# Gated activations of 27 chunks transposed by DMA instead of by TensorE

## The chip, the cores and the metric

The kernel runs on one core of a Trainium2 chip. The metric is the device time of one execution in microseconds (us), lower is better. Three executions of the kernel before took 380.42, 380.49 and 380.88 us, median 380.49.

## The reference

Attention with spatially reduced keys, and behind it a mixture of eight low-rank adapters. Cut to what matters:

```python
B, C, H, W = 4, 128, 384, 32             # q: (B, 12288, 128), kv: (B, 384, 32, 128)
kv_pool = kv.reshape(B, H//4, 4, W//4, 4, C).mean(axis=(2, 4))
k = v = kv_pool.reshape(B, -1, C) @ w_sr                       # 768 keys a batch
a = softmax(q @ k.T / sqrt(C))
x = (a @ v).reshape(-1, C)                                     # 49152 tokens
logits = x @ w_gate                                            # 8 experts
# the two best experts of a token get softmax weights w; for each of them:
x += w * ((x @ A[e]) @ B[e])                                   # rank 16
```

## The kernel before, in words

**Tiles.** The 49152 tokens are worked on in 96 chunks of 512 (24 a batch). A chunk's scores are three units, each two matmuls of 128x512 into a tile `sg` and one exponential on ScalarE into `em` (L294). The attention product is 24 matmuls into `acc`; the routing logits come out of the same matmuls as extra columns of the values. VectorE normalizes into `xn` (reciprocal L315, product L320) and finds the best two logits (L340); GpSimd forms the gates `gw` (L352 to L368) with a tanh on ScalarE (L365).

**The adapters of one chunk.** All eight experts' low-rank matrices are taken together as one 128x128 matrix. A chunk's `xn` is transposed on TensorE into `tt_ps` and copied by VectorE to `tts` (L389, function `transposes`); `down` multiplies it into `h_ps`; `gate` multiplies by the gates on VectorE into `hg` (L420); `hg` is transposed in turn, in the other half of the same `tt_ps`, in the next slot; `up` multiplies it into `d_ps`; `finish` adds `xn` on VectorE into `osb` (L433) and issues the output's DMA on the SP queue (L434). Four matmuls each for a transpose, `down` and `up`. `tt_ps`, `h_ps`, `d_ps` and the tiles of the key preparation share two PSUM buffers (`mtile`).

**Slots.** After an opening written out by hand, one loop runs over slots k = 8 to 95. Slot k does the three score units of chunk k, attends chunk k-1, normalizes the chunk attended before, and, for the one chunk x that *enters* (`enter[k]`, x = k-4 in the slots concerned), the transposes of `xn` and the down-projection. `kh` holds the chunk whose gated activations are transposed in this slot (it entered a slot ago), `ku` the one that gets its up-projection (it entered two slots ago). The order in a slot is that of the code, kept on every engine's queue.

**What `begin(k)` issues.** On the SP queue the transposing load of 2048 queries, `load_qT` (L90), in the slots of `loads` (10, 14, 18, ... 62, then 61 and 63 to 67 for the last batch's groups); on GpSimd's queue the cast of a group of queries to bf16 in DRAM, `cast_q` (L80, tile `qbf`), in the slots of `casts` (8, 12, 15, 16, 19, 20, 23, 24, 28, ...); and on SP the loads of the next batch's keys, `load_kv` (L102), in slots 3 to 14 of the first batch and 0 to 11 of the second and third.

**The late chunks.** Chunks 68 to 89 already have both transposes done by DMA: GpSimd narrows `xn` to bf16 (L403), the gate writes beside it, and one DMA transpose on SP (`turn_dma`, L407, tile `turn`) turns both.

The times at which slots 14 to 18 start their score units in the trace are some 3.6 to 4.1 us apart; the name "slot 18" below is that of k = 18 (normalization at 86.22 us).

Of the kernel before, what the change touches and what calls it, by code (L numbers as in the profile page):

```python
# [11 lines left out]
BF16 = mybir.dt.bfloat16  # L12
# [8 lines left out]
def kernel(  # L21
# [10 lines left out]
    nc = tc.nc  # L32
    P = 128
# [6 lines left out]
    S = T // P  # L40
# [5 lines left out]
    NB = N // T  # L46
# [11 lines left out]
    gpool = ctx.enter_context(tc.tile_pool(name="gpool", bufs=6))  # L58
    run = ctx.enter_context(tc.tile_pool(name="run", bufs=3))
    opool = ctx.enter_context(tc.tile_pool(name="opool", bufs=8))  # L60
    qdram = ctx.enter_context(tc.tile_pool(name="qdram", bufs=1, space=bass.MemoryType.DRAM))
    ps_s = ctx.enter_context(tc.tile_pool(name="ps_s", bufs=2, space=bass.MemoryType.PSUM))
    ps_a = ctx.enter_context(tc.tile_pool(name="ps_a", bufs=1, space=bass.MemoryType.PSUM))
# [2 lines left out]
    keep = tc.keep_in_program_order  # L66

    def mm(*a, **k):
        return keep(nc.tensor.matmul(*a, **k))  # L69

    def mtile(shape, dtype=FP32, name="mb"):
        return ps_m.tile(shape, dtype, tag="mb", name=name)
# [10 lines left out]
    def load_qT(g):  # L83
        if g < B * NG - GC:
            t = qpool.tile([P, GT], BF16, tag="qT", name="qT")
        else:
            if "q" not in spare:
                spare["q"] = kvpool.tile([P, 4, 2, 4 * C], FP32, tag="kvr", name="qTs")
            t = spare["q"][:, g % GC].rearrange("p x c -> p (x c)").bitcast(BF16)
        keep(nc.sync.dma_start(t.rearrange("c (j p) -> c j p", p=P),  # L90
                               q_bf[g].rearrange("(p j) c -> p (j c)", p=P), transpose=True))
        qT[g] = t
# [190 lines left out]
    tts, xT, hgT, hp, hg, dp = {}, {}, {}, {}, {}, {}  # L283
    R = J // 2

    def scores(k, r):
        b = k // NB
        if k not in em:
            em[k] = ppool.tile([P, J, T], FP16, tag="em", name="em")
        rhs = qT[k // GC][:, (k % GC) * T:(k % GC + 1) * T]  # L290
        ps = ps_s.tile([P, 2, T], FP32, tag="sg", name="sg")
        for i in range(2):
            mm(ps[:, i], kfT[b][:, 2 * r + i], rhs, start=True, stop=True)
        keep(nc.scalar.activation(em[k][:, 2 * r:2 * r + 2], ps, AF.Exp, bias=0.0, scale=scale))  # L294
# [31 lines left out]
    SOLO, TURN = NCHUNK - 6, NCHUNK - 28  # L326
    sizes = [1, 1] + [2] * (TURN // 2 - 1) + [1] * (NCHUNK - TURN)
    by_dma = range(TURN, SOLO)
# [66 lines left out]
    def strip(t, i):  # L395
        if "t" not in spare:
            t_ = kvpool.tile([P, 4, 2, 4 * C], FP32, tag="kvr", name="turn")
            spare["t"] = t_.rearrange("p r x c -> p (r x c)").bitcast(BF16).rearrange(
                "p (n t h s c) -> p n t h s c", n=4, t=2, h=2, s=S)
        return spare["t"][:, t % 4, i]  # L400

    def narrow(k, t):
        keep(nc.gpsimd.tensor_copy(strip(t, 0)[:, 0], xn[k][:, :, 0:C]))  # L403

    def turn_dma(t, *what):
# [3 lines left out]
        for i, (d, k) in enumerate(what):  # L409
            d[k] = strip(t, 1)[:, lo + i]  # L410

    def down(k):
        hp[k] = mtile([P, S, P], name="h_ps")
        for s in range(S):
            mm(hp[k][:, s], xT[k][:, s], a_bf, start=(s == 0), stop=(s == S - 1))

    def gate(k, into=None):
        k0, m = first[k], k - first[k]
        hg[k] = run.tile([P, S, P], BF16, tag="hg", name="hg") if into is None else into
        keep(nc.vector.tensor_tensor(  # L420
            hg[k].rearrange("p s (e r) -> p (s e) r", e=E),
            hp[k].rearrange("p s (e r) -> p (s e) r", e=E),
            gw[k0][:, m * S:(m + 1) * S].rearrange("p s e -> p (s e)")
            .unsqueeze(2).broadcast_to([P, S * E, RK]), op=ALU.mult))
# [33 lines left out]
    def unit(k=None, r=None):  # L458
        k, r = units.pop(0 if k is None else units.index((k, r)))
        scores(k, r)  # L460
# [3 lines left out]
    loads = {4 * g - 6: g for g in range(4, 18)}  # L464
    loads.update({61: 20, 63: 21, 64: 18, 65: 22, 66: 19, 67: 23})
    assert len(casts) == B * NG - 4

    def begin(k):
        nonlocal sums, rest
        b, i = divmod(k, NB)  # L470
        g = k // GC
        if k in loads:
            load_qT(loads[k])
        if k in casts:
            cast_q(4 + casts.index(k))
        if b + 1 < B:
            lo = 3 if b == 0 else 0
            if i == lo:
                sums, rest = prepare(b + 1, nc.gpsimd)
                sums = sum(sums, [])  # L480
            if lo <= i < 12 + lo:
                load_kv(b + 1, (i - lo) // 4, (i - lo) % 4, None)
        if k == 7:
            for _ in range(2):
                sums.pop(0)()
# [11 lines left out]
    enter, t, left = {}, 1, list(range(NCHUNK - 3))  # L497
    while left:
        can = [k for k in left if ready[k] <= t]
        enter[t] = can[:2] if t == SOLO + 2 else can[:1]  # L500
        left = [k for k in left if k not in enter[t]]
        t += 1

    kh, ku, kd, kdone = [], [], [], []
    engines = {"DVE": nc.vector, "ACT": nc.scalar, "POOL": nc.gpsimd}
# [40 lines left out]
    kh, ku = enter[k1 - 1], enter[k1 - 2]  # L546
    for k in range(k1, NCHUNK):
        b, i = divmod(k, NB)
        ka = att.get(k, [])
        kx = enter.get(k, [])  # L550
        begin(k)

        def after_norm(kn):
            top(kn)
            if kn == first[kn] + size[kn] - 1:
                route(first[kn])

        kn = [n for n in att.get(k - 1, []) if normed[n] == k]
        unit()
        if kx and not kd and all(x_ in by_dma for x_ in kx):  # L560
            down(kx[0])
            todo = []
            for n in kn:
                normalize(n)
                if n in by_dma:
                    narrow(n, k)
                    todo = [(xT, n)]
            tanhs()
            for h_ in kh:
                if h_ not in by_dma:  # L570
                    transposes(None, h_, nc.vector)
            unit()
            gate(kx[0], strip(k, 0)[:, 1])
            todo.append((hgT, kx[0]))
            if len(kx) == 1:
                turn_dma(k, *todo)
            for u_ in ku:
                up(u_)
                finish(u_)
            attend(ka[0], 0)  # L580
            attend(ka[0], 1)
            unit()
            for n in kn:
                after_norm(n)
            attend(ka[0], 2)
            for x_ in kx[1:]:
                down(x_)
                gate(x_, strip(k, 0)[:, 0])
                turn_dma(k, (hgT, x_), *todo)
            attend(ka[0], 3)  # L590
            kh, ku = kx, kh
            continue
        tanhs()
        for x_ in kd:
            down(x_)
        for n in kn:
            normalize(n)
            if n in by_dma:
                narrow(n, k)
                turn_dma(k, (xT, n))  # L600
        px, ph = ([c for c in ks if c not in by_dma] for ks in (kx, kh))
        pairs = [(px[j] if j < len(px) else None, ph[j] if j < len(ph) else None)
                 for j in range(max(len(px), len(ph)))]
        for x_, h_ in pairs[:1]:
            transposes(x_, h_, nc.vector)
        for x_ in kd:
            gate(x_)
        unit()
        for u_ in ku:
            up(u_)  # L610
            finish(u_)
        for a_ in ka[:-1]:
            for s in range(S):
                attend(a_, s)
            normalize(a_)
            after_norm(a_)
        if ka and len(ka) == 1:
            attend(ka[0], 0)
        for n in kn:
            after_norm(n)  # L620
        if k >= 13:
            unit()
            n0 = 1
        else:
            attend(ka[0], 1)
            n0 = 2
        for x_ in kx[:1]:
            down(x_)
            gate(x_)
        kd = []  # L630
        if rest and i in ((14, 15, 16, 18, 19, 20, 21, 22, 23) if b == 0 else (11, 12, 13, 17, 18, 19, 21, 22, 23)):
            rest.pop(0)()
        for a_ in ka[-1:]:
            for s in range(n0 if len(ka) == 1 else 0, S):
                if s == S - 1:
                    for x_, h_ in pairs[1:]:
                        transposes(x_, h_, nc.scalar)
                        kd = [x_] if x_ is not None else []
                attend(a_, s)
        ku = kh  # L640
        kh = kx[:1] + kdone
        kdone = kd
        if b + 1 < B and i % 2 == 0 and (8 if b == 0 else 6) <= i <= 20:
            for _ in range(4 if (b, i) == (0, 18) else 3):
                sums.pop(0)()
# [185 lines left out]
```

## Time and profile before

| what | value |
|---|---|
| runs, median (lowest to highest) | 380.49 us (380.42 to 380.88) |
| profiled execution, span from the first to the last instruction | 379.1 us |
| median less that span | 1.4 us |
| ScalarE, GpSimd busy | 293.3 us (77%), 217.8 us (57%) |
| DMA moved | 82.22 MB, mean 217 GB/s |
| DMA queue of SP (q1), share of 16 engines | 69.8% |
| DMA queue of GpSimd's casts (q0) | 17.0% |

The profile is of one execution, and its times are counted from the first instruction; for that execution no device time apart from its span is listed, so the runs' median stands beside it. Each engine runs its own instructions in order. "L69" is a helper's line through which every matmul goes, so TensorE's rows are told apart by their tiles. SP only issues DMAs; its rows give how long an issue held it, and "to landing" is the time from the start of the issue until all data has arrived.

### The profile page before, as it was taken

To read this page: it belongs to the slowest core of one execution; us is meant where nothing else is said; L and a number is where in the kernel's file an instruction comes from. 1 tells how busy PE (TensorE), PEld (TensorE's weight loads), DVE (VectorE), ACT (ScalarE), POOL (GpSimd) and SP (SyncE) were. 2 spreads that over 40 slices of the span, in tenths; PEclk is the share of its full clock that TensorE was granted. 3 is DMA by queue.
4 is the path that set the end of the run, shared out by engine and by line. 5 is a ranking of instruction groups with operands and counts; after the bars stand their busy time and mean duration, and the time that the engine had idled before them with its cause. 6 is when DMAs were issued, how large, how long until landed. Compare 5 with 4: busy or idle time off the path is not lost.

```text
span 379.1 us, 11473 instructions
## 1 busy us (share of the span) xinstructions
PE 368.8 (97%) x4448; PEld 292.5 (77%) x4448; DVE 307.6 (81%) x925; ACT 293.3 (77%) x368; POOL 217.8 (57%) x493
## 2 busy tenths in 40 slices
PE   8899999999999999999999999999999999999993
PEld 5577788788788887878788887878787777777782
DVE  1447799998989889898989888898988777777785
ACT  1448986776878788787878787777778999999873
POOL 0120468878732387777833267777675666666442
PEclk9999999999999999999999999999999999999998
DMA  7988979999999998997898998989955867777623
GB/s 247 388 291 151 279 184 266 340 224 241 152 213 228 299 278 268 255 235 165 171 201 226 288 239 245 306 233 198 217 137 140 169 163 153 150 205 168 141 86 140
DMA packets 93863, 82.22 MB, mean 217 GB/s; under 512 B 73104, under 2 KB 73872, under 8 KB 93456
## 3 DMA queue, kind: packets, MB, share of 16 engines
q1 hardware_dynamic: 92672, 69.75, 69.8%
q0 software_dynamic: 704, 11.54, 17.0%
q8 instruction: 35, 0.57, 0.6%
q10 hardware_dynamic: 432, 0.20, 0.2%
q14 instruction: 20, 0.16, 0.2%
HBM read 50.53 MB, written 36.70 MB: 230 GB/s over the span
## 4 chain that ended last, share of the span: by engine, by line
PE 91%; DMA 4%; DVE 2%; issue 1%; ACT 1%; SPq 0%; POOL 0%; ACTq 0%; DVEq 0%; POOLq 0%
PE acc L69 35%; PE sg L69 32%; PE tt_ps L69 8%; PE d_ps L69 5%; PE h_ps L69 5%; DMA kvr<-in_kv_dram 4%; PE kpT_ps L69 2%; PE v_ps L69 1%; DVE kvr L135 1%; DVE xn L320 1%; PE kfT_ps L69 1%; DMA out_dram<-osb 1%; PE qT_ps L69 0%; SPq L102 0%; PE tail_ps L69 0%
## 5 line engine op out<-in xcount | busy, mean ns | idle before, releaser
L294 ACT ACTIVATE em<-sg 128x1024 f16<-128x1024 f32 x288 | 282.4, 1022 | 66.8 <-PE sg L69 64.1
L69 PE MATMUL acc<-vx,em 128*128 128x136 f16 x2280 | 166.5, 223 | 0.0
L69 PEld LDWEIGHTS <-em 128*128 128x128 f16 x2304 | 145.2, 98 | 7.7 <-DVE xn L320 0.4
L69 PE MATMUL sg<-qT,kfT 128*128 128x512 bf16 x480 | 142.1, 379 | 0.8 <-ACT em L294 0.7
L320 DVE TENSOR_TENSOR xn<-acc,rinv 128x540 f32<-128x540 f32 x95 | 68.4, 720 | 3.3
L69 PEld LDWEIGHTS <-tts 128*128 128x128 bf16 x564 | 43.0, 98 | 31.6 <-issue 0.4
L223 POOL TENSOR_TENSOR kvr<-kvr 128x512 f32<-128x512 f32 x54 | 67.3, 1270 | 0.1
L352 POOL TENSOR_TENSOR over<-xn,srt 128x64 f32<-128x64 f32 (+1 forms) x120 | 30.9, 278 | 55.4 <-DVE srt L340 55.3
L433 DVE TENSOR_TENSOR osb<-d_ps,xn 128x512 f32<-128x512 f32 x91 | 62.5, 688 | 0.0
L420 DVE TENSOR_TENSOR hg<-h_ps,gw 128x512 bf16<-128x512 f32 x71 | 49.0, 691 | 6.3 <-POOL gw L368 1.2
L389 DVE COPY tts<-tt_ps 128x1024 bf16<-128x1024 bf16 (+1 forms) x73 | 49.0, 672 | 0.0
L69 PEld LDWEIGHTS <-kfT 128*128 128x128 bf16 x576 | 45.3, 98 | 2.7 <-issue 1.0
L315 DVE RECIPROCAL rinv<-acc 128x4 f32<-128x4 f32 x95 | 17.3, 182 | 36.9 <-PE acc L69 35.9
L367 POOL TENSOR_TENSOR gw<-th,over 128x64 f32<-128x64 f32 (+1 forms) x60 | 17.3, 288 | 49.6 <-ACT th L365 47.4
L69 PEld LDWEIGHTS <-xn 128*128 128x128 bf16 x296 | 22.5, 98 | 16.7 <-DVE xn L320 0.4
L340 DVE MAX8 srt<-xn 128x8 f32<-128x8 f32 x380 | 34.4, 152 | 0.1
L69 PE MATMUL sg<-qTs,kfT 128*128 128x512 bf16 x96 | 28.6, 379 | 0.0
L69 PE MATMUL tt_ps<-id_bf,xn 128*128 128x128 bf16 x284 | 27.4, 219 | 0.0
L69 PE MATMUL h_ps<-a_bf,tts 128*128 128x128 bf16 x284 | 27.4, 219 | 0.0
L69 PE MATMUL tt_ps<-id_bf,hg 128*128 128x128 bf16 x280 | 27.1, 219 | 0.0
L69 PE MATMUL d_ps<-b_bf,tts 128*128 128x128 bf16 x276 | 26.7, 219 | 0.1
L358 POOL TENSOR_SCALAR over<-over 128x64 f32<-128x64 f32 (+1 forms) x60 | 19.8, 330 | 5.4
(93 smaller groups left out, 280.7 us busy)
## 6 DMA issues: line engine op xcount, KB each, us to landing
out_dram<-osb SPq DMA_DIRECT2D x94, 256.0 KB, 4.3
kvr<-in_kv_dram SPq DMA_DIRECT2D x45, 512.0 KB, 7.8
qbf<-in_q_dram POOLq DMA_DIRECT2D x22, 512.0 KB, 7.7
qf<-in_q_dram SPq DMA_DIRECT2D x8, 256.0 KB, 7.4
kvr<-in_kv_dram SPq DMA_DIRECT2D x6, 256.0 KB, 7.8
out_dram<-osb SPq DMA_DIRECT2D x3, 128.0 KB, 2.3
turn<-turn SPq DMA_TRANSPOSE x23, 3.1
qT<-qbf SPq DMA_TRANSPOSE x18, 7.4
```

What stands on the lines that cost most here:

```text
L69: return keep(nc.tensor.matmul(*a, **k))
L223: keep(adder.tensor_tensor(u[:, lo:hi], u[:, lo:hi], v[:, lo:hi], op=ALU.add))
L294: keep(nc.scalar.activation(em[k][:, 2 * r:2 * r + 2], ps, AF.Exp, bias=0.0, scale=scale))
L315: keep(nc.vector.reciprocal(ri, acc[k][:, :, VC]))
L320: keep(nc.vector.tensor_tensor(x[:, :, 0:VC], acc[k][:, :, 0:VC], ri.unsqueeze(2).broadcast_to([P, S, VC]), op=ALU.mult))
L340: keep(nc.vector.max(srt[k0][:, m, s], xn[k][:, s, C:C + E]))
L352: keep(eng.tensor_tensor(d, lg, so[:, :, i].unsqueeze(2).broadcast_to([P, n, 8]), op=ALU.subtract))
L358: keep(eng.tensor_scalar(mask, mask, 0.0, None, op0=ALU.is_ge))
L367: keep(eng.tensor_tensor(w[:, 0:n], th, mask, op=ALU.mult))
L389: keep(nc.vector.tensor_copy(sb[:, lo:hi], ps[:, lo:hi]))
L420: keep(nc.vector.tensor_tensor(hg[k].rearrange("p s (e r) -> p (s e) r", e=E), hp[k].rearrange("p s (e r) -> p (s e) r", e=E), gw[k0][:, m ...
L433: keep(nc.vector.tensor_tensor(osb, dp[k], xn[k][:, :, 0:C], op=ALU.add))
```

## The change

In 27 slots (13 to 23 of the first batch, 37 to 47 of the second, 61 to 65 of the third) the chunk that enters gets its gated activations turned by a DMA of its own, `turn_h_dma`, issued on SP right behind the gate, from a tile `hs` into a tile `ht` (a pool of four each). TensorE's transposes of `hg` and their half of VectorE's copy fall away for them. Their up-projection moves from the slot k+2 to k+3 (`late_up`), with the addition and the output behind it. A query load of such a slot is issued behind this transpose, at the end of the slot; in the other slots it goes from ahead of to behind the key load and the first score unit.

```diff
+    hpool = ctx.enter_context(tc.tile_pool(name="hpool", bufs=4))
...
+    def turn_h_dma(k):
+        hgT[k] = hpool.tile([P, S, P], BF16, tag="ht", name="ht")
+        keep(nc.sync.dma_start(hgT[k].rearrange("c s p -> c s p"),
+                               hg[k].rearrange("p s c -> p (s c)"), transpose=True))
...
-    def begin(k):
+    def begin(k, queries=True):
...
-        if k in loads:
+        if k in loads and queries:
             load_qT(loads[k])
...
+    by_queue = [k for t in range(8, TURN - 2) if t % NB >= 13 for k in enter[t]]
+    late_up = {}
...
-        begin(k)
+        begin(k, False)
...
         unit()
+        if k in loads and not any(x_ in by_queue for x_ in kx):
+            load_qT(loads[k])
+        ku = ku + late_up.pop(k, [])
...
-        px, ph = ([c for c in ks if c not in by_dma] for ks in (kx, kh))
+        px = [c for c in kx if c not in by_dma]
+        ph = [c for c in kh if c not in by_dma and c not in by_queue]
...
             down(x_)
-            gate(x_)
+            if x_ in by_queue:
+                gate(x_, hpool.tile([P, S, P], BF16, tag="hs", name="hs"))
+                turn_h_dma(x_)
+                late_up[k + 3] = [x_]
+                if k in loads:
+                    load_qT(loads[k])
+            else:
+                gate(x_)
...
-        ku = kh
+        ku = [c for c in kh if c not in by_queue]
```

More of the change, by code (lines that the diff above doesn't have):

```diff
@@ L590 @@
             attend(ka[0], 3)
-            kh, ku = kx, kh
+            kh, ku = kx, [c for c in kh if c not in by_queue]
             continue
```

## The prediction

> **What bounds the kernel now.** I read the page first, then the timeline of one slot on TensorE and VectorE, then the DMA answers. The page's own rows for the engines and for the transposes that the change takes away:
>
> ```profile
> span 379.1 us, 11473 instructions
> PE 368.8 (97%) x4448; PEld 292.5 (77%) x4448; DVE 307.6 (81%) x925; ACT 293.3 (77%) x368; POOL 217.8 (57%) x493
> L69 PE MATMUL tt_ps<-id_bf,hg 128*128 128x128 bf16 x280 | 27.1, 219 | 0.0
> ```
>
> TensorE is busy for 97% of the span, but a matmul's duration (219 ns) is its way through the array and overlaps its neighbours, so the price of an edit is read from starts. One slot on TensorE (slot 18, start us, then duration):
>
> ```profile
> 85.80 0.59 PE L69 MATMUL sg<-qT,kfT 128*128 128x512 bf16 x2
> 86.24 0.39 PE L69 MATMUL tt_ps<-id_bf,xn 128*128 128x128 bf16 x4
> 86.46 0.39 PE L69 MATMUL tt_ps<-id_bf,hg 128*128 128x128 bf16 x4
> 86.68 0.59 PE L69 MATMUL sg<-qT,kfT 128*128 128x512 bf16 x2
> 87.11 0.39 PE L69 MATMUL d_ps<-b_bf,tts 128*128 128x128 bf16 x4
> ...
> 89.64 0.59 PE L69 MATMUL sg<-qT,kfT 128*128 128x512 bf16 x2
> ```
>
> Each group starts when the one before has been fed; no gap stands between them. The four transposes of gated activations run from 86.46 to 86.68: 0.22 us, not the 0.39 of their row. The slot lasts 89.64 - 85.80 = 3.84 us. In the late slots, where both kinds of transposes already go by DMA, the same slot start recurs after 3.16 us, and ScalarE's three exponentials fill about that much:
>
> ```profile
> 297.87 0.59 PE L69 MATMUL sg<-qT,kfT 128*128 128x512 bf16 x2
> 301.03 0.59 PE L69 MATMUL sg<-qT,kfT 128*128 128x512 bf16 x2
> 299.54 3.15 ACT L294 ACTIVATE em<-sg 128x1024 f16<-128x1024 f32 x3
> ```
>
> So ScalarE would limit a slot at about 3.16. The plain slot at the start of the second batch lasts 3.61 (120.58 less 116.97, quoted further down). One transpose group less makes 3.39: still TensorE's, and 0.22 is really won per slot. VectorE's copy in slot 18 of the transposes (first row) shrinks by the half that went away, so VectorE, 81% busy, does not become the bound:
>
> ```profile
> 86.88 0.69 DVE L389 COPY tts<-tt_ps 128x1024 bf16<-128x1024 bf16 x1
> 87.54 0.69 DVE L433 TENSOR_TENSOR osb<-d_ps,xn 128x512 f32<-128x512 f32 x1
> ```
>
> **The change part by part.** The chunks that enter in slots 13-23, 37-47 and 61-65 are 11 + 11 + 5 = 27.
>
> Removed: 27 groups of transposes by 0.22 = 5.9 us, all on the path, in slots 14-24, 38-48 and 62-66.
>
> Added on TensorE: nothing, but the up-projection comes three slots after the chunk's down-projection instead of two. So slots 15, 39 and 63 have none and slots 26, 50 and 68 have two. The second one there needs the PSUM buffer that the transposes used, which is free when VectorE has copied them. In slot 26:
>
> ```profile
> 116.97 0.39 PE L69 MATMUL tt_ps<-id_bf,xn 128*128 128x128 bf16 x4
> 117.85 0.39 PE L69 MATMUL d_ps<-b_bf,tts 128*128 128x128 bf16 x4
> 120.58 0.39 PE L69 MATMUL tt_ps<-id_bf,xn 128*128 128x128 bf16 x4
> 117.61 0.69 DVE L389 COPY tts<-tt_ps 128x1024 bf16<-128x1024 bf16 x1
> ```
>
> A second group would start 0.22 behind 117.85, at 118.07; the copy ends at 118.30. Some 0.3 us each, 3 x 0.3 = 0.9 (0 if other work slides in between, 1.8 if VectorE's extra 0.69 for the second output also shows).
>
> Added on SP and the DMA queue: 27 transposes of 512 columns behind the gate, then in slots 14, 18, 22, 38, 42, 46 and 61-65 the query transpose of 2048 columns behind them. The nearest rows (count, then us to landing; below them one issue of each on SP, start and duration):
>
> ```profile
> turn<-turn SPq DMA_TRANSPOSE x23, 3.1
> qT<-qbf SPq DMA_TRANSPOSE x18, 7.4
> 293.39 1.24 SPq L407 DMA_TRANSPOSE turn<-turn  x1
> 72.79 4.54 SPq L90 DMA_TRANSPOSE qT<-qbf  x1
> ```
>
> The late `turn` has 1024 columns in most slots, so half of it holds SP about 0.6 us (an estimate: half of 1.24) and lands within 3.1. The gate of slot k ends about 3.0 us after the slot's normalization, and the up-projection that needs the turned data starts some 8 us later (three slots of 3.39, less 2.2 of one). Undisturbed, 3.1 against 8 is no wait. That is the cover, and the question is what breaks it. Queued behind the new wait on SP are the output of the next slot and the query load; both have slots in hand, the query load about four. TensorE takes its instructions in order, so a turned tile that is late stops everything.
>
> The breaker is in the DMA answers. GpSimd's query casts move 32 KB packets, and while they run nothing of SP's queue moves. The window 96.0 to 100.6, with one output issued at 96.2 waiting in it:
>
> ```profile
> DMA packets 31, 0.49 MB, mean 107 GB/s; under 512 B 16, under 2 KB 16, under 8 KB 16
> q0 software_dynamic: 31, 0.49, 61.3%
> out_dram<-osb SPq DMA_DIRECT2D x1, 256.0 KB, 8.9
> ```
>
> There is no row of SP's queue q1 at all, and that output needed 8.9 us (the third row is from the window 96.1 to 96.3). The Trainium skill ("DMA: Bandwidth & Descriptors", Queues, rings and completion order) says that each DMA engine round-robins between its queue rows packet by packet. The window does not agree for a pair of casts: no packet of q1 came between.
>
> Two places decide, each with a pair of casts just where the query transpose of the slot before stands ahead of the new transpose. **First, slots 14-18.** The casts are issued here:
>
> ```profile
> 76.87 0.58 POOL L80 DMA_DIRECT2D qbf<-in_q_dram  x1
> 78.86 0.57 POOL L80 DMA_DIRECT2D qbf<-in_q_dram  x1
> qbf<-in_q_dram POOLq DMA_DIRECT2D x1, 512.0 KB, 6.1
> qbf<-in_q_dram POOLq DMA_DIRECT2D x1, 512.0 KB, 9.1
> out_dram<-osb SPq DMA_DIRECT2D x1, 256.0 KB, 10.2
> out_dram<-osb SPq DMA_DIRECT2D x1, 256.0 KB, 9.2
> 73.33 0.69 DVE L420 TENSOR_TENSOR hg<-h_ps,gw 128x512 bf16<-128x512 f32 x1
> 77.10 0.69 DVE L420 TENSOR_TENSOR hg<-h_ps,gw 128x512 bf16<-128x512 f32 x1
> ```
>
> The landing rows are of the casts at 76.87 and 78.86 (they land at 83.0 and 88.0) and of the outputs issued at 78.1 and 80.9 (land 88.2 and 90.1): SP's transfers land right behind the cast. In slot 14 the gate ends at 74.0, and only then does the query transpose start, which started at 72.79 before and was through ahead of the casts. It holds SP at least 4.5 us, to 79; the chunk gated in slot 15 (ended 77.8) is issued after that, into the casts, behind the query's remaining data. It lands between those two outputs, middle 89.1. Its up-projection is in slot 18, where 87.11 (quoted) less five transpose groups (1.1) and less one missing up-projection (0.2) makes 85.8. TensorE waits 89.1 - 85.8 = 3.3 us by the end of slot 18 (2.4 to 4.3), part of it perhaps already in slot 17.
>
> **Second, slots 38-42**, the same pattern (the casts issued at 167.2 and 169.2, the second one's landing, an output issued at 170.4, the query transpose on SP, the gate of slot 39, the up-projection of slot 42; the last row is that of slot 22, used below):
>
> ```profile
> qbf<-in_q_dram POOLq DMA_DIRECT2D x1, 512.0 KB, 7.9
> out_dram<-osb SPq DMA_DIRECT2D x1, 256.0 KB, 7.3
> 159.86 5.49 SPq L90 DMA_TRANSPOSE qT<-qbf  x1
> 167.04 0.69 DVE L420 TENSOR_TENSOR hg<-h_ps,gw 128x512 bf16<-128x512 f32 x1
> 176.66 0.39 PE L69 MATMUL d_ps<-b_bf,tts 128*128 128x128 bf16 x4
> 102.78 0.39 PE L69 MATMUL d_ps<-b_bf,tts 128*128 128x128 bf16 x4
> ```
>
> The query transpose moves from 159.86 to about 164.4, so 5.5 of it would hold SP to 169.9 and 3 of it to 167.4. The turned chunk of slot 39 (gate ended 167.7) is then issued into the casts and lands as the output at 170.4 did, 177.7. It is needed at 176.66 - 1.3 = 175.4: 2.3 us (0 if it gets through ahead of the first cast, 2.5 else).
>
> The other pairs (issued in slots 19/20, 23/24, 43/44, 47/48) come out within a microsecond of the need: for slot 22, the output issued at 96.2 landed at 105.1, against an up-projection that stood at 102.78, less 2.2 saved, plus 3.3 of shift, 103.9. I take 0.3 for each of the four and 0.1 for slots 64-68, together 1.3 (0 to 6); in 64-68 the query loads follow one another, but no cast is left, and I reckon each chunk to land 1 to 4 us ahead.
>
> Sum: -5.9 + 0.9 + 3.3 + 2.3 + 1.3 = +1.9. The sum is on the traced execution's span, 379.1; the runs' median is 380.49, and the 1.4 us outside the span is carried over. 380.5 + 1.9 = **382.4**.
>
> **The rivals.**
>
> *Every turned tile arrives in time.* Then only the 5.9 and the 0.9 count: 375.5, faster. For it: 3.1 us to land against 8. Against it: outputs on the same queue needed 9 to 10 us beside casts. It decides at slot 18: if the chunk of slot 15 lands before 85.8, this is what happens. 0.17.
>
> *SP's queue gets a turn between two casts.* A transpose then waits one packet, not two: slot 42 costs nothing and slot 18 its lower end, 2.4: -5.9 + 0.9 + 2.4 + 1.3 = -1.3, 379.2, faster. For it: the two casts at 76.87 and 78.86 landed at 83.0 and 88.0, which leaves room between them. Against it: the window quoted. 0.14. The round-robin rule of the Trainium skill named above speaks for this case.
>
> *Only slot 18 waits*: the chunk of slot 39 slips through. -5.9 + 0.9 + 3.3 + 1.3 = -0.4: 380.1, no change. 0.08.
>
> *The casts catch every run.* At slots 22, 26, 46 and 50 the wait is 1.5 instead of 0.3: +4.8, 387.2. For it: each pair can hold the queue for over 6 us, and a query transpose is just ahead in three of the four. Against it: as reckoned, TensorE has shifted by then and the need comes later. 0.16.
>
> *The change does not shorten TensorE's slot*, as another engine is the limit: excluded as far as 3.16 against 3.39 goes.
>
> **How the numbers follow.** My case has 0.45, with its own range 380.9 to 385.5; some 0.06 of it lies within 0.2% (0.76 us, about what can be told from no change). Faster: 0.17 + 0.14 = 0.31. Same: 0.08 + 0.06 = 0.14. Slower: 0.39 + 0.16 = 0.55. The range 376.0 to 387.0 leaves out about half of the first rival and the upper half of the fourth, under 2 in 10.
>
> **What would show it.** Right: slots without query loads or casts start 3.39 apart; TensorE idle ahead of `d_ps` in slots 17-18 and 42, ended by the DMA of the turned tile, 2 to 4 us each, several us in all; new transposes whose median landing is near 3 to 6 us but whose longest is 9 or more. Wrong: no wait of TensorE on that tile (then 375.5); waits mainly in slots 64-68, where I see none; slots that do not shrink by 0.22; or waits on query tiles.

## The result: 16 us slower, in turned tiles that land behind casts

| what | before | after |
|---|---|---|
| runs, median (lowest to highest, count) | 380.64 us (380.24 to 381.01, 6) | 396.43 us (393.54 to 415.56, 6) |
| profiled execution: time, span | span 379.1 us | 398.34 us, 396.6 us |

The ratio of the times is 1.0379, with an interval of 1.0352 to 1.0406; it leaves out the two longest runs of the changed kernel (406.05 and 415.56), as every ratio below leaves out a kernel's runs of over 1.5% above its shortest, and none is given where only one run was left. The forecast was 382.4 with a range of 376.0 to 387.0: the sign was right, the size was not.

From the page of the kernel after (span, busy time of the engines, chain of work by engine and by line):

```profile
span 396.6 us, 11321 instructions
PE 369.8 (93%) x4340; PEld 288.9 (73%) x4340; DVE 300.6 (76%) x925; ACT 294.3 (74%) x368; POOL 218.3 (55%) x493
PE 77%; DMA 17%; DVE 3%; ACT 1%; issue 1%; SPq 0%; POOL 0%; ACTq 0%; DVEq 0%; POOLq 0%
```

The same chain line of the kernel before:

```profile
PE 91%; DMA 4%; DVE 2%; issue 1%; ACT 1%; SPq 0%; POOL 0%; ACTq 0%; DVEq 0%; POOLq 0%
```

The path that sets the end went from TensorE to the DMAs, 4% to 17%. The view of waits of the kernel after names the tile (us in total, times, longest; PEld is TensorE's weight load, which waits for the same tile and is not added):

```profile
PEld L70 <- DMA ht<-hs: 18.4, 8, 5.5
PE d_ps L70 <- DMA ht<-hs: 14.7, 6, 5.0
```

Six up-projections waited 14.7 us in all for a turned tile, and the timeline of TensorE says which (the wait in brackets):

```profile
80.16 0.40 PE L70 MATMUL d_ps<-b_bf,ht 128*128 128x128 bf16 x4 [1.39 <-DMA ht<-hs]
88.12 0.40 PE L70 MATMUL d_ps<-b_bf,ht 128*128 128x128 bf16 x4 [4.29 <-DMA ht<-hs]
89.90 2.25 PE L70 MATMUL acc<-vx,em 128*128 128x136 f16 x18
94.72 1.23 PE L70 MATMUL acc<-vx,em 128*128 128x136 f16 x18
109.54 0.40 PE L70 MATMUL d_ps<-b_bf,ht 128*128 128x128 bf16 x4 [0.53 <-DMA ht<-hs]
188.13 0.61 PE L70 MATMUL d_ps<-b_bf,ht 128*128 128x128 bf16 x4 [5.00 <-DMA ht<-hs]
214.43 0.40 PE L70 MATMUL d_ps<-b_bf,ht 128*128 128x128 bf16 x4 [1.86 <-DMA ht<-hs]
219.83 0.40 PE L70 MATMUL d_ps<-b_bf,ht 128*128 128x128 bf16 x4 [1.61 <-DMA ht<-hs]
```

These are slots 16, 17, 22, 42, 48 and 49. The lengths of the slots, each from one start of the normalization to the next in the timeline of VectorE (us; "no casts" is the changed kernel without the casts, the second experiment):

| slot | before | after | no casts |
|---|---|---|---|
| 16 | 3.78 | 5.06 | 3.59 |
| 17 | 3.55 | 9.40 | 3.42 |
| 22 | 4.12 | 4.60 | 4.00 |
| 24, 38, 40 (nothing else in them) | 3.61 | 3.48 | 3.48 |
| 26, 50, 68 (two up-projections) | 3.61 | 4.12 | 4.12 |
| 42 | 4.12 | 10.54 | 4.00 |
| 48, 49 | 3.61, 3.61 | 5.41, 5.40 | 3.48, 3.61 |
| 39 (no up-projection) | 3.61 | 3.48 | 3.48 |
| slots 12 to 79, in all, against before | 0 | +17.5 | -1.6 |

So the six slots with waits are 18.3 us longer than without casts (1.47 + 5.98 + 0.60 + 6.54 + 1.93 + 1.79), which is nearly all of the 17.5 + 1.6 = 19.1.

That is more than their 14.7 us of waiting. In the two rows of 18 attention matmuls above, the first took 2.25 us and the second 1.23. Stretches of the span around them (length, busy time of the five engines, then granted clock, DMA share, GB/s):

```profile
83.90:88.10 4.20, 0.00 (x0) 0.00 (x0) 0.15 (x1) 1.25 (x2) 0.00 (x0) 1.00 0.69 133
88.10:92.00 3.90, 3.88 (x35) 3.37 (x36) 1.66 (x6) 1.02 (x1) 1.25 (x4) 0.59 0.97 221
92.50:96.00 3.50, 3.50 (x45) 2.83 (x43) 2.96 (x10) 3.00 (x4) 1.84 (x4) 1.00 0.63 189
```

TensorE idles for 4.2 us, then works 3.9 us at a granted clock of 0.59, then at 1.00. Behind the wait of 5.00 (188.1 to 192.0) it is 0.60 for 3.9 us. Work at 0.59 for 3.9 us loses 3.9 x 0.41 = 1.6 us, and that much is missing: slot 17 grew by 5.98 for a wait of 4.29, slot 42 by 6.54 for one of 5.00, 1.5 to 1.7 us more each. Slot 48 grew by 1.93 for a wait of 1.86, so the short waits have no such tail. The Trainium skill ("TensorE: Matmul & The Clock Gate", Part 1) says that the clock falls to half after an idle window of about 3.4 us and returns after about as much sustained work; the three stretches agree.

**Why the tiles are late.** SP's and VectorE's timelines at the first run (the last row is VectorE's gate of slot 14):

```profile
66.74 4.70 SPq L103 DMA_DIRECT2D kvr<-in_kv_dram  x1
73.40 1.66 SPq L415 DMA_TRANSPOSE ht<-hs  x1
77.26 1.26 SPq L415 DMA_TRANSPOSE ht<-hs  x1
78.69 8.98 SPq L91 DMA_TRANSPOSE qT<-qbf  x1
87.79 1.19 SPq L415 DMA_TRANSPOSE ht<-hs  x1
...
72.58 0.69 DVE L426 TENSOR_TENSOR hs<-h_ps,gw 128x512 bf16<-128x512 f32 x1 [0.28 <-POOL gw L369]
```

Slot 14's gate ended at 73.3 (forecast 74.0), but its transpose was issued at 77.26: SP was four microseconds behind, having been held 4.70 us by one key load (the key loads issued between 62 and 67 us held it 0.54 to 0.87 in the kernel before). So it went out beside the casts issued at 76.2 and 78.2. From the DMA views of short windows around single issues (us to landing: this tile, the second cast beside it; then of the second run the tile issued at 174.81, the casts issued at 174.20 and 176.20, the query transpose issued at 172.52):

```profile
ht<-hs SPq DMA_TRANSPOSE x1, 10.8
qbf<-in_q_dram POOLq DMA_DIRECT2D x1, 512.0 KB, 9.2
ht<-hs SPq DMA_TRANSPOSE x1, 13.3
qbf<-in_q_dram POOLq DMA_DIRECT2D x1, 512.0 KB, 8.3
qbf<-in_q_dram POOLq DMA_DIRECT2D x1, 512.0 KB, 11.6
qT<-qbf SPq DMA_TRANSPOSE x1, 13.6
```

77.26 + 10.8 = 88.1, and the cast lands at 87.4. 174.81 + 13.3 = 188.1, and the cast lands at 187.8. In slots 48 and 49 it is the same: a tile lands 0.2 to 0.3 us behind a cast. It is not so in slots 16 and 22: the tile of slot 16 landed at 80.1, ahead of both casts, after 6.7 us (6.4 without casts, experiment 2), and that of slot 22 at 109.5, between its two casts (106.2 and 111.4). At the second run the casts, too, are longer than before, 8.3 and 11.6 us. Of the same pair in the kernel before the second took 7.9 (its row is in the prediction), and the first:

```profile
qbf<-in_q_dram POOLq DMA_DIRECT2D x1, 512.0 KB, 6.0
```

The DMA queues in two windows of the second run, 174 to 176 (first row, only SP's queue, both transposes) and 180 to 184 (packets, MB, share of 16 engines):

```profile
q1 hardware_dynamic: 1662, 0.43, 113.1%
...
q0 software_dynamic: 19, 0.43, 94.1%
q1 hardware_dynamic: 213, 0.05, 9.0%
```

SP's queue moved 1662 packets in 2 us, then 213 in 4 us, while the casts were in flight (the first landed at 182.5). Of all 27 tiles (view by tile: SP's hold in ns, then the landing):

```profile
L415 SPq DMA_TRANSPOSE ht<-hs x27: 1189/1260/5555, 73.4 to 285.0; - x27
DMA to landing us min/median/max: 2.4/5.9/13.3
```

A turned tile holds SP for 1.2 us at least; the estimate was 0.6.

**Why the gain is smaller.** The lengths above give 0.13 us a slot, not 0.22. TensorE and ScalarE in slot 62 of the kernel after:

```profile
266.80 0.59 PE L70 MATMUL sg<-qT,kfT 128*128 128x512 bf16 x2
268.11 0.52 PE L70 MATMUL acc<-vx,em 128*128 128x136 f16 x6
268.57 0.59 PE L70 MATMUL sg<-qT,kfT 128*128 128x512 bf16 x2
267.49 1.02 ACT L295 ACTIVATE em<-sg 128x1024 f16<-128x1024 f32 x1 [0.86 <-PE sg L70]
```

The score units have two buffers. The unit at 268.57 writes where the exponential begun at 267.49 reads until 268.51, and starts just then: with a group less ahead of it, it came to that wait. And slots 26, 50 and 68 pay 0.51 each for the second up-projection, here in slot 26:

```profile
124.36 0.39 PE L70 MATMUL d_ps<-b_bf,tts 128*128 128x128 bf16 x4
124.88 0.38 PE L70 MATMUL d_ps<-b_bf,ht 128*128 128x128 bf16 x4
```

It starts 0.52 behind the first: 0.22 for a group, as in the prediction, and the 0.3 of waiting. Slot 39, which has no up-projection, is no shorter than its neighbours (table), so the 0.22 is not given back there.

### The profile page after: what moved, and what is told of

The parts are those of the page before. It is cut to its first block, busy times and chain, and to the rows that moved or that the text cites. A ratio compares the mean times of both kernels' runs of the same rounds, so it can differ in the third digit from the quotient of the medians.

```text
span 396.6 us, 11321 instructions
## 1 busy us (share of the span) xinstructions
PE 369.8 (93%) x4340; PEld 288.9 (73%) x4340; DVE 300.6 (76%) x925; ACT 294.3 (74%) x368; POOL 218.3 (55%) x493
## 4 chain that ended last, share of the span: by engine, by line
PE 77%; DMA 17%; DVE 3%; ACT 1%; issue 1%; SPq 0%; POOL 0%; ACTq 0%; DVEq 0%; POOLq 0%
PE acc L70 31%; PE sg L70 27%; DMA ht<-hs 13%; PE tt_ps L70 5%; PE d_ps L70 5%; PE h_ps L70 5%; DMA kvr<-in_kv_dram 3%; PE kpT_ps L70 2%; PE v_ps L70 1%; DVE xn L321 1%; DVE tts L390 1%; DVE kvr L136 1%; ACT em L295 1%; PE kfT_ps L70 0%; PE qT_ps L70 0%
## 5 line engine op out<-in xcount | busy, mean ns | idle before, releaser
L70 PEld LDWEIGHTS <-tts 128*128 128x128 bf16 x456 | 35.1, 99 | 25.9 <-issue 1.2
L368 POOL TENSOR_TENSOR gw<-th,over 128x64 f32<-128x64 f32 (+1 forms) x60 | 17.4, 290 | 51.3 <-ACT th L366 49.2
L390 DVE COPY tts<-tt_ps 128x1024 bf16<-128x1024 bf16 (+1 forms) x73 | 41.6, 570 | 0.0
L426 DVE TENSOR_TENSOR hg<-h_ps,gw 128x512 bf16<-128x512 f32 x44 | 30.4, 691 | 3.9 <-POOL gw L369 1.5
L426 DVE TENSOR_TENSOR hs<-h_ps,gw 128x512 bf16<-128x512 f32 x27 | 18.7, 692 | 8.6 <-PE h_ps L70 3.2
L70 PE MATMUL d_ps<-b_bf,ht 128*128 128x128 bf16 x108 | 10.7, 223 | 15.2 <-DMA ht<-hs 14.7
L70 PEld LDWEIGHTS <-ht 128*128 128x128 bf16 x108 | 7.8, 99 | 23.0 <-DMA ht<-hs 18.4
```

The costliest lines, as they stand in the source:

```text
L368: keep(eng.tensor_tensor(w[:, 0:n], th, mask, op=ALU.mult))
L390: keep(nc.vector.tensor_copy(sb[:, lo:hi], ps[:, lo:hi]))
L426: keep(nc.vector.tensor_tensor(hg[k].rearrange("p s (e r) -> p (s e) r", e=E), hp[k].rearrange("p s (e r) -> p (s e) r", e=E), gw[k0][:, m ...
```

## The experiments

The theory after the result: SP's transposing DMAs (turned tiles, and query transposes in their new places) and GpSimd's casts meet, and each waits for the other. Rivals: SP's own backlog would do it without casts; the new order of the query loads alone does it; a slot more of time would do. The expectations stand as they were written, each with the theories of its moment.

**1, 2. No casts.** From the seventh group on the casts are left out, and the query loads read the groups cast at the start. The same edit in the kernel before and in the kernel after:

```diff
     def cast_q(g):
+        if g >= 6:
+            q_bf[g] = q_bf[4 + g % 2]
+            return
```

> The kernel before with GpSimd's casts of the query groups 6 to 23 left out (their query loads read the cast groups 4 and 5 again, so 18 of 22 casts are missing and those chunks get other queries). It is the partner of nocast_after. Every theory: about as the kernel before, 378 to 381, since TensorE sets its pace; faster only if the casts cost something there already.

> The changed kernel with the same casts left out (queries of groups 4 and 5 read again). Theory (the turned tiles are late because the casts and the new transposes meet in the DMA engines): no wait of TensorE on the turned tile over 1 us, and the time 1 to 3 us below nocast_before (27 slots by 0.13, less about 0.5 at each of the three double up-projections). Rival (SP's queue by itself is too full, the query load ahead of the new transpose): waits stay at slots 16 to 17 and 42, and the time is at least 5 us above nocast_before.

Before: 380.53 us, ratio 1.0003 (0.9991 to 1.0015). After: 380.00, ratio 0.9994 (0.9984 to 1.0004). The waits on turned tiles are gone; the view by tile of the second:

```profile
DMA to landing us min/median/max: 2.4/3.2/6.4
```

16 us shrink to nothing. So the loss needs the casts: SP's backlog without them is harmless (a key load held SP for 3.79 us there too, and the tile of slot 14 went out 0.9 us behind its gate). With the casts their bytes are gone as well, so this pair does not say which of the two counts. What is left of the change is a gain of some 0.5 us, smaller than expected, which asks for the third experiment.

**3. The third score unit behind the down-projection**, without casts, so that it does not come to the exponential's buffer too early:

```diff
+        behind = any(c in by_queue for c in kh)
         if k >= 13:
-            unit()
+            if not behind:
+                unit()
...
+        if behind:
+            unit()
```

> nocast_after, and in the 27 slots without transposes of gated activations the third score unit is put behind the down-projection. Theory (the slot only shrank by 0.13 of 0.22 because the third score unit waits for the first exponential to free one of two score buffers): the slot goes from 3.48 to about 3.39, some 2.4 us below nocast_after. Rival (another limit of the slot, such as the accumulator's release or VectorE): no change within 0.5 us, or slower.

377.10 us (376.66 to 377.86), ratio 0.9918 (0.9901 to 0.9936): 2.9 us below the second kernel. The timeline of TensorE shows the order:

```profile
170.16 0.39 PE L70 MATMUL d_ps<-b_bf,ht 128*128 128x128 bf16 x4
170.39 0.52 PE L70 MATMUL acc<-vx,em 128*128 128x136 f16 x6
170.74 0.39 PE L70 MATMUL h_ps<-a_bf,tts 128*128 128x128 bf16 x4
170.96 0.59 PE L70 MATMUL sg<-qT,kfT 128*128 128x512 bf16 x2
```

The ordinary slot is now 3.38 us, where the prediction had 3.39. The missing 0.1 a slot came of the order of the units, as the wait for the exponential would have it.

**4. Query transposes first**, in their old places at the slot's start, with the turned tiles as they are:

```diff
-        begin(k, False)
+        begin(k)
...
-                if k in loads:
-                    load_qT(loads[k])
```

> The changed kernel with the query load put back to the slot's beginning, ahead of the key load and of the gate, as before the change. Theory (casts): the query transpose of slot 38 is through before the casts, so the wait at slot 42 mostly goes; at slots 16 to 17 the new transpose of slot 14 now stands behind the query load and is still caught by the casts: 384 to 390. Rival (the query load's late place is the whole cause): 378 to 382. Rival (order does not matter): as the changed kernel, 393 or more.

405.75 us, ratio 1.0656 (1.0627 to 1.0685): worse than the change. Only the last rival's "393 or more" covers the number, and not its reason, that order does not matter. The waits of TensorE:

```profile
PE d_ps L70 <- DMA ht<-hs: 25.3, 5, 10.1
```

The turned tile then stands behind the query transpose and still beside the casts: being last on SP costs more than being ahead.

**5. A slot more of time**: the up-projection a further slot later (`late_up[k + 4]` for `late_up[k + 3]`).

> The changed kernel with the up-projection of the 27 chunks one slot later still (four slots behind the entry instead of three). Theory (tiles are late behind a pair of casts by a limited time): the cover grows from about 8 to 11.5 us against landings of at most 13.3 in the changed kernel, so waits shrink to 0 to 2 us at slots 17 to 18 and 42 to 43 and go elsewhere: 381 to 386. Rival (SP's queue falls behind for good there): still 390 or more.

403.72 us (393.21 to 419.62): the theory missed, and the rival's number came. In its profiled execution, the shortest at 393.21, the waits shrink to 6.8 us, but tiles still land up to 12.4 us after their issue, and the total is about the shortest of the change, 393.54. A slot more of time is no remedy.

**6. No query transposes beside the tiles**: in the new slots of the first two batches the query load is left out (the chunks take the group before).

> The changed kernel with the six query loads of slots 14, 18, 22, 38, 42 and 46 left out (their chunks use the queries of the group before). It asks whether the casts alone make the tiles late or only with a query transpose queued ahead. Theory (both: a pair of casts stops the queue for about 6 us, and the 2048-column transpose adds its own 2 to 9 us on SP): waits of TensorE on the turned tile fall to 0 to 2 us a place: 382 to 386. Rival A (the casts alone do it): as the changed kernel, 392 or more. Rival B (the query transposes alone do it): no waits at all, 380.

393.40 us (383.09 to 398.36): one execution fits the theory, three are longer (390.62 and more). In the profiled one, the shortest, the turned tiles cost little: 3.4 us of waits, though they land after up to 11.8 us. Of the longer ones there is no trace, so whether turned tiles alone make the loss stays open.

**7, 8. Casts moved** out of the slots with turned tiles (7), and with experiment 3's order and the second up-projection behind the gate beside it (8; the second up-projection moves in 11, 12 and 16 too):

```diff
-    casts = sorted([k for k in range(8, 61, GC)] + [15, 19, 23, 39, 43, 47])
+    casts = [8, 9, 11, 12, 24, 26, 28, 30, 32, 34, 35, 36, 48, 50, 52, 53, 54, 56, 58, 59]
```

> The changed kernel with GpSimd's 20 casts at other slots, none in 13 to 23 and 37 to 47: 8, 9, 11, 12, then 24 to 36 and 48 to 59, beside the key loads. Theory: no wait of TensorE on the turned tile over 1 us, 379 to 381, as without the casts. Rival (the DMA engines are simply full, and what is late moves with the casts): key loads come late, GpSimd's sums and the key preparation with them, 384 or more.

> castmoved, with the third score unit behind the down-projection in the slots without transposes of gated activations, and the second up-projection of slots 26, 50 and 68 behind the gate. Theory: 0.1 us less in some 24 slots and 0.3 in three: 3 to 3.5 us below castmoved, 376 to 377.5, faster than the kernel before. Rival (key loads late): as castmoved's rival.

429.29 us, ratio 1.1187 (1.1166 to 1.1209; the profiled execution was the longest, 469.93), and 435.50, ratio 1.1205 (1.1136 to 1.1275). The turned tiles now land after 2.4 to 9.2 us and still cost 11.0 us of waits, but the casts met the query transposes (54.9 us of waits). TensorE's timeline of 7, then its DMA view of the window 282 to 300:

```profile
310.57 1.03 PE L70 MATMUL sg<-qT,kfT 128*128 128x512 bf16 x2 [36.46 <-DMA qT<-qbf]
```

```profile
DMA packets 805, 0.61 MB, mean 34 GB/s; under 512 B 764, under 2 KB 764, under 8 KB 794
q1 hardware_dynamic: 774, 0.24, 98.6%
q0 software_dynamic: 31, 0.36, 23.2%
```

The query transpose issued at 259.2 landed after 51.3 us, and the four casts beside it after 35.8 to 40.7. In this window the packets of SP's queue are recorded with 0.986 x 18 x 16 / 774 = 0.37 us each on average; in the window 174 to 176 of the kernel after, with no cast's packet in it, with 1.131 x 2 x 16 / 1662 = 0.022 (with shares of over 100% the records overlap, so this is no rate). The whole core moved 34 GB/s. In this one execution, then, both kinds get slow together. It is not the same everywhere: in the window 180 to 184 of the kernel after SP's packets are few but short (0.09 x 4 x 16 / 213 = 0.027), and long ones come without casts too: in the kernel of experiment 2 the window 76.3 to 78 has 91 packets, 57.4% and no cast, 0.17 us each.

**9, 12. Smaller cast packets**, 4 KB instead of 32 (12: with experiment 3's order and the second up-projection at the end of the slot), to let SP's packets in more often:

```diff
-        keep(nc.gpsimd.dma_start(t, q[g // NG, (g % NG) * GT:(g % NG + 1) * GT]))
+        keep(nc.gpsimd.dma_start(
+            t.rearrange("(a b r) c -> b a (r c)", a=8, b=16),
+            q[g // NG, (g % NG) * GT:(g % NG + 1) * GT].rearrange("(a b r) c -> b a (r c)", a=8, b=16)))
```

> The changed kernel with each of GpSimd's casts cut into 128 pieces of 4 KB output instead of 16 of 32 KB, the same bytes. Theory (a transposing DMA and a cast in flight together wait for each other packet by packet, so a 256-byte packet of the transpose lasts as long as a cast packet, up to 2.4 us): packets of some 0.3 us make the collision cheap, the waits on the turned tile go to 0 to 2 us in all, 379 to 384. Rival (the DMA engines have too many bytes to move there, whatever the packets): as the changed kernel, 392 or more; more descriptors could make it worse.

> smallcast, with the third score unit behind the down-projection and the second up-projection behind the gate. Theory: 27 slots by 0.23, less what waits are left: 3 us below smallcast, 376 to 381. Rival (bytes): 389 or more.

399.48 us (390.71 to 403.2) and 394.40, ratio 1.0343 (1.0314 to 1.0372): the theory missed in both. In the trace of 9 tiles still land up to 13.9 us after their issue, and casts up to 15.0. With packets of 4 KB the loss stays, so the 32 KB are not what makes it.

**10. The tiles moved, but not transposed**: the new DMA copies `hs` to `ht` as it is.

> The changed kernel with the 27 new DMAs as plain copies from hs to ht, the same bytes without the transpose (the up-projection of those chunks then takes untransposed data). Theory (it is the transposing that falls into step with the casts): a plain copy is only held back while a cast runs, up to about 6 to 9 us against 8 of cover, so waits are 0 to 2 us at each of the two or three places, and the query transposes still meet the casts: 381 to 388. Rival (any transfer on SP's queue beside a pair of casts comes as late): 392 or more.

392.86 us, ratio 1.0305 (1.0284 to 1.0327): the theory missed, and the rival came. TensorE's waits:

```profile
PE d_ps L70 <- DMA ht<-hs: 10.2, 4, 5.3
```

They are on the copied tiles. That of slot 14 was issued at 74.85, ahead of the cast at 76.03, and landed with it, after 11.9 us. The query transposes, later than before, still met the casts: the one of slot 14 landed after 14.8 us. So a tile need not be transposed to come too late.

**13. Both**: tiles copied (10) and no query transposes beside them (6), all casts in place.

> The changed kernel without the six query loads of noq and with the 27 new DMAs as plain copies as in plain (queries of the group before, untransposed data in the up-projection): no transposing DMA is left beside the pairs of casts. Theory (each transposing DMA in flight beside casts, query or turned tile, makes both slow): no waits over 1 us, 379.5 to 381.5. Rival (casts alone, or the bytes of 27 more transfers): still 386 or more.

383.00 us (379.87 to 386.62), ratio 1.0040 (1.0000 to 1.0081): between the theory and its rival, and nearer the theory. The waits of TensorE:

```profile
PE d_ps L70 <- DMA ht<-hs: 1.5, 3, 1.1
```

All casts but the early ones landed in 5.2 to 8.4 us. Against 10 (ratios 1.0305 and 1.0040) only the six query loads are gone, so with copied tiles they make most of the loss. Their bytes (512 KB each) and their time on SP's queue are gone with their transposing; no run loads the queries without it, so which of these counts is not shown. Against 6 nothing is told: its shortest execution, 383.09, lies within the executions of 13.

**11. Only the chunks of slots 61 to 71**, where hardly a cast is left, with experiment 3's order.

> The change made only where no cast is in flight: the chunks that enter in slots 61 to 71 (57 to 67; six of them new, between the last cast and the late chunks), with the third score unit behind the down-projection and second up-projections behind the gate. Theory: 11 slots by 0.23 less some 0.2 where up-projections double: 2.0 to 2.6 us below the kernel before, 378.0 to 378.7. Rival (seven query transposes in a row fill SP's queue, so that turned tiles are late there too): 380 or more.

383.24 us, ratio 1.0074 (1.0042 to 1.0106): the theory missed. The profiled execution was its longest, 399.64 us, and in it the waits are not on turned tiles in the main:

```profile
PE sg L70 <- DMA qT<-qbf: 10.5, 3, 5.7
```

They are in slots 20, 28 and 44, where nothing is turned. What still differs there from the kernel before is the place of the query load.

**14, 15. That place alone.** 14 is the kernel before with its query loads behind the key load and the first score unit, and nothing else; 15 is the kernel after with the old place in all slots but the 27.

```diff
-        if k in loads:
-            load_qT(loads[k])
...
         unit()
+        if k in loads:
+            load_qT(loads[k])
```

> The kernel before with one part of the change alone: every query load issued behind the key load and the first score unit of its slot instead of ahead of them; no new DMA, TensorE's transposes as before. Theory (a query transpose that starts a microsecond later runs into the casts of slots 15, 19, 23 and so on): query loads land 15 us and more after their issue in some slots, 382 to 390. Rival (only the new transposes matter; last11 was slow by itself): 380 to 381.

> The changed kernel with the query loads of the slots outside the 27 (10, 26, 30, 34, 50, 54, 58, 66, 67) back ahead of the key load. Theory (the order outside those slots is a small part; the turned tiles and the query loads behind them collide): 389 to 396. Rival (the order of the other slots is the main cause): 384 or less.

14: 388.13 us (379.6 to 394.43). The DMA view around the query load of slot 14, and the wait of TensorE:

```profile
qT<-qbf SPq DMA_TRANSPOSE x1, 24.0
PE sg L69 <- DMA qT<-qbf: 4.7, 1, 4.7
```

In the profiled execution (387.50 us) it was issued at 74.1 instead of 72.79 and landed after 24.0 us, where the kernel before needs 10.4; slot 20 is 7.4 us longer. But the shortest execution of 14 is as short as the kernel before, and of that kernel's 23 executions beside it four took 388.08 to 410.69. So it is not shown that this order costs by itself.

15: 403.31 us (392.44 to 411.66); the shortest lies within the expected 389 to 396, the others above. To take the order back does not help where the tiles are turned. Its trace (404.49 us) shows one thing more. The tile of slot 14 was issued at 74.23, 1.2 us behind its gate and ahead of both casts (75.90 and 77.89). It landed after 16.6 us, at 90.8, as the second cast did at 91.0. TensorE waited for it longer than in the kernel after:

```profile
90.87 0.61 PE L70 MATMUL d_ps<-b_bf,ht 128*128 128x128 bf16 x4 [8.98 <-DMA ht<-hs]
```

So to be issued ahead of the casts does not save a tile.

**16. The smallest version**: only slots 61 to 65, experiment 3's order, the query loads of all other slots in the old place.

> The change made only for the five chunks that enter in slots 61 to 65, where no cast is in flight, with the third score unit behind the down-projection, the second up-projection of slot 68 behind the gate, and the query loads of all other slots in the order of the kernel before. Theory: 5 slots by 0.23 less 0.2 in slot 68: 1.0 below the kernel before, 379.2 to 380.0. Rival (turned tiles late in slots 64 to 68 behind the query transposes): 380.5 or more.

380.06 us (379.01 to 382.86), ratio 0.9988 (0.9971 to 1.0006): not told from no change. Its slots 62 to 66 are 0.22 to 0.33 us shorter, and slot 67 is 0.84 longer for a wait on a tile: what is left of the change where no casts are is little.

## Why the prediction was right in sign and wrong in size

**Right.** Slots 17 and 42 are where the two long waits are, on the up-projection, ended by the turned tile, with casts as the cause; there were no waits in slots 64 to 68; the second up-projection's stall was 0.3. Of the signs named for "wrong", one came: slots that do not shrink by 0.22. That slot 17 waits was right in place and cause, but not by the chunk that was reckoned.

**Wrong, term by term.** *Removed:* 3.2 us instead of 5.9, about 0.13 in each of the 27 slots without casts but slot 45, which is 0.12 longer. "0.22 is really won per slot" was reckoned from ScalarE's total of 3.16 a slot; that is a throughput, and the third unit's wait for a buffer is an order. *Double up-projections:* 3 x 0.51 instead of 3 x 0.3; the group itself (0.22) was taken to be made up in the slot without one, and it is not. Together the change without casts is worth 1.5 us in the profiles of experiments 1 and 2 (1.6 less 0.1) and 0.5 in the medians, instead of 5.0.

*Slots 14 to 18:* 3.3 us were reckoned for the chunk of slot 15, "issued after that, into the casts". By the time that one landed, TensorE had been stopped by the one before it: the chunk of slot 14, which the prediction let go out ahead of the casts at its gate's end, and for which it reckoned no wait of its own (only "part of it perhaps already in slot 17"). This is the failed step. In the kernel after SP issued it 4 us behind the gate, and it landed after 10.8 us; in experiment 15 it went out ahead of both casts, as reckoned, and landed after 16.6. So its place on SP is only half of it: the prediction had no term for a transfer that is issued ahead of the casts and lands only with them. The trace of the kernel before had one to show: the query transpose "through ahead of the casts", issued at 72.79, landed after 10.4 us, at 83.2, 0.2 behind the first cast. That the chunk of slot 15 landed at 90.3 (forecast 89.1) is luck: it was issued only at 87.79, when the query transpose had held SP for 8.98 us (4.5 reckoned) and both casts were in, and it then needed 2.5 us. With the idle tail at the lower clock, slots 16 and 17 cost 7.5 us.

*Slots 38 to 42:* 2.3 us (0 to 2.5) were reckoned from an output's landing and the casts' old length; the wait was 5.0 and the slot 6.5 longer, since the casts took 8.3 and 11.6 us. The step that failed here takes the casts for a block of the length that they had before. *The other pairs:* slots 48 and 49 cost 3.7 us, 22 another 0.6, against 1.2 for four. The rival in which the casts catch every run (387.2) had the right kind of outcome, and its sizes too low for the same reasons. The rival in which the queue gets a turn between two casts is out at the two long waits: both tiles landed behind the second cast.

**Not in the sum at all:** the clock after a long wait, 1.5 to 1.7 us each.

**Shown, and open.** That the loss needs the casts is shown by 2, and that with copied tiles most of it needs the six query loads beside them by 13 against 10. Whether turned tiles alone make it (6), and whether the transposing counts or the bytes, is open. That casts and SP's DMAs can both become slower together is seen in the landings of 7 and 14, in one execution each. Why these DMAs disturb each other was not settled; with smaller cast packets (12) the loss stays. Nor was it settled why executions of one kernel differ so much: the changed kernel's by 22 us, and now and then those of the kernel before, too.

## What to carry to other kernels

Before work is moved from a compute engine to a DMA, list what else is in flight on the DMA engines between its issue and its deadline, and price it by the worst landing of that stretch; the median of a quiet stretch (here 3.1 us) says nothing of it. A transfer that is issued ahead of the others is not safe from them. Reckon the issue from the queue's timeline, not from the moment when the data is ready. And take a slot's gain from the next wait in its order, not from the busy time of the next engine.

## What the runs showed of the hardware

- A DMA transpose and a cast in DRAM, in flight together, can both take much longer. A 512-column transpose landed after 2.4 to 6.4 us without casts (experiment 2) and up to 13.3 in the kernel after; a query transpose from slot 14 on after 4.6 to 6.6 without casts (experiment 1), 5.4 to 10.9 in the kernel before and 24.0 in experiment 14; a cast after 5.5 to 9.4 us in the kernel before, 11.6 in the kernel after and 21.5 in experiment 14.
- In the window 176 to 180 of the kernel after the DMA view counts 29 packets of the casts' queue and 612 of SP's, of 21 KB and 0.25 KB on average. The Trainium skill ("DMA: Bandwidth & Descriptors", Queues, rings and completion order) has the queues take turns by packets; packets of both moved here, but 29 to 612 is not one turn of the view's packets for one.
- A 512-column transpose holds SP as long as one of 1024 columns, 1.2 us.
- A wait of 4.29 us costs TensorE 5.98, one of 1.86 costs 1.93: the granted clock is 0.59 for 3.9 us behind the long one.
